# Two token tiles transposed by the matmul engine, and weight pieces moved out of the early tiles

## The chip, the cores and the metric

The kernel runs on one core of one Trainium2 chip. The metric is the device time of one execution in microseconds. The engines are PE (matmul), ACT (scalar), DVE (vector), POOL (gpsimd) and SP (here it only issues DMAs); each runs its own instruction stream, and semaphores order them against each other.

## The reference

Three layers follow each other: windowed attention with a summary of every block, a dense two-layer MLP, and a mixture of 8 experts of which every token takes one. The last is what the change is about:

```python
def _moe2_ref(x, w_gate, w1, w2):            # x 1536x512, w1 8x512x1024, w2 8x1024x512
    logits = x @ w_gate
    expert_idx = np.argmax(logits, axis=1)
    ...
    for e in range(E):
        mask = expert_idx == e
        ...
        h = np.maximum(x[mask] @ w1[e], 0.0)
        out[mask] = gate_w[mask, None] * (h @ w2[e])
```

With the inputs of these runs the experts get 879, 426, 168, 62 and 1 tokens, and three get none.

## The kernel before

The tokens form 12 tiles of 128 (u = 0 to 11). Float32 values are kept as a high and a low float16 part, so a product is three matmuls. `x2_out(u)` takes the finished sum of the dense layer of tile u (`x2ps`, PSUM), makes the two parts `x2c` (ACT L518 the high, DVE L519 the low), transposes them by DMA into `x2t` and stores them in `x2d` in DRAM. `gate(u)` multiplies `x2t` by the gate weights (L537, 12 matmuls into `pl`), finds the expert of every token and its slot by some 20 short DVE operations and one ACT operation, and POOL writes token number and gate value into `tbl`. A planner's list of positions (`at`) sets the order in which the program is written here, and within it the framework schedules each engine's stream.

The mixture follows in `sparse()`. The experts are ranked; (v, j) is tile j of the expert of rank v. The expert of rank 0 has 426 tokens, three full tiles and a half tile of 64 or fewer; rank 1 has seven full tiles; ranks 2 to 4 have one full tile and a half one, a half one, a half one. Three tiles of rank 0, (0,0) to (0,2), are the early tiles: they run on tables made before the last gates, and an If (`redo`, L886) repeats them when too few tokens were known. Then come `last_half(0)`, a chain of branches (`go`, L877) for further tiles of rank 0 that is jumped over here, `full(1, 0)`, and `chain(1, 1)` for (1,1) to (1,6); the ranks behind follow.

`s_tile` is one tile: 96 matmuls L715 into two PSUM halves `hp`, after each half ACT L719 and DVE L720 make `hh`, then (`work`) the weight pieces, then 24 matmuls L734 into `yp` (L730 for a half tile), ACT L737 scales it to `y`, and POOL L740 writes the rows to `out_dram`. `gather` and `h_gather` get a tile's rows: POOL L685 gathers from `x2d` into `xr`, and SP L687 transposes by DMA into `xa`, `xb`, `xe` or `xh`.

An expert's weights come in 8 pieces of 512 KB. Piece g belongs to the expert of rank g // 8. `piece(g)` splits it from one of five buffers `raw0` to `raw4` into two float16 parts (`s_split`: ACT L197, then DVE L198), and then has SP load piece g + 5 into the buffer it freed (`s_load`, L661 and L664). The buffers hold pieces 22 (= SOON) to 26 when the early tiles begin: 22 in `raw2`, 23 in `raw3`, 24 in `raw4`, 25 in `raw0`, 26 in `raw1`. `prep(lo, hi)` is the list of pieces lo to hi - 1, and `beside[j]` the first piece that is done in tile (1, j). `prep_x(r)` gathers the first tiles of rank r and loads the table of rank r + 1. On ACT and DVE a tile with `work` keeps the written order.

## Time and profile before

| what | value |
|---|---|
| median of 3 runs | 565.43 us (564.78 to 569.46) |
| the profiled execution | 564.62 us, of which 562.8 us from the first to the last instruction |
| mean granted PE clock | 0.926 |
| PE busy | 476.8 us, 85% of the span |
| DVE, ACT, POOL busy | 303.6, 264.0 and 223.2 us |
| DMA | 87.49 MB, 155 GB/s in the mean |

The profiled execution is 0.81 us under the median. Starts are in microseconds from the begin of the span. [...]

### The profile page before, as it was taken

The page shows a single profiled execution, that of the slowest core. Times are in us where ns is not written, and L with a number is a line of the kernel's source. Part 1 is how long each engine was busy: PE and PEld are TensorE (multiplying, and loading weights), DVE is VectorE, ACT ScalarE, POOL GpSimd, SP SyncE. Part 2 cuts the span into 40 slices and gives each one's busy share as a digit, 9 for nine tenths or more (in the row PEclk, how much of TensorE's full clock was granted, in tenths as well). Part 3 has the DMA queues.
Part 4 walks back from the last instruction along what each step waited for, and adds up shares of the span by engine and source line. Part 5 has one row for each costly group of instructions (what it writes and reads, how often), then busy time and mean ns, then how long its engine had stood idle before and what let it go on. Part 6 is the DMA issues. An engine that isn't in the chain of part 4 may idle for free.

```text
span 562.8 us, 12709 instructions
## 1 busy us (share of the span) xinstructions
PE 476.8 (85%) x4792; PEld 325.2 (58%) x4792; DVE 303.6 (54%) x778; ACT 264.0 (47%) x559; POOL 223.2 (40%) x217
## 2 busy tenths in 40 slices
PE   5726957969899999999999997989938799996971
PEld 2315844847556555686587476547617476775650
DVE  5999699998972233573354268865332344310110
ACT  3777685877774233356266235644132344321110
POOL 3476765777674113465156206501301332210110
PEclk9856995899999999999999998999988899997997
DMA  8997967995650454714351558884394999940310
GB/s 276 263 249 200 322 192 165 207 232 162 180 139 0 76 94 108 158 40 88 83 94 24 103 155 254 270 254 127 131 174 86 271 278 324 207 124 21 46 35 7
DMA packets 114775, 87.49 MB, mean 155 GB/s; under 512 B 85199, under 2 KB 94671, under 8 KB 114688
## 3 DMA queue, kind: packets, MB, share of 16 engines
q1 hardware_dynamic: 104656, 65.27, 48.2%
q10 hardware_dynamic: 7056, 13.11, 7.8%
q0 software_dynamic: 2976, 8.01, 4.6%
q8 instruction: 47, 0.77, 0.6%
q14 instruction: 40, 0.33, 0.2%
HBM read 57.29 MB, written 7.97 MB: 116 GB/s over the span
## 4 chain that ended last, share of the span: by engine, by line
PE 31%; DMA 30%; DVE 16%; issue 16%; POOL 2%; ACT 2%; SPq 1%; POOLq 1%; another core or an unknown queue 0%; ACTq 0%; DVEq 0%
PE x2ps L510 16%; PE hps L490 11%; DMA xr<-x2d,tbh 7%; DMA out_dram<-y,tbe 6%; DMA xr<-x2d,tb 4%; DMA stg<-in_moe_w_in_dram 2%; DMA tbl<-row,slot 2%; DVE yps L234 2%; DVE y L238 2%; DVE yps L236 2%; DVE s L401 2%; DMA pt<-pb 2%; DVE kb L198 2%; PE ps L385 2%; PE po L443 1%
## 5 line engine op out<-in xcount | busy, mean ns | idle before, releaser
L490 PE MATMUL hps<-xt,wih 128*128 128x256 f16 x768 | 137.0, 283 | 10.4 <-DVE rel L496 5.7
L510 PE MATMUL x2ps<-wo,gt 128*128 128x512 f16 x576 | 131.2, 380 | 0.0
L490 PE MATMUL hps<-xt,wil 128*128 128x256 f16 x384 | 108.8, 283 | 2.8 <-POOL wil L247 2.8
L490 PEld LDWEIGHTS <-wih 128*128 128x128 f16 x768 | 76.7, 102 | 24.8 <-issue 4.7
L510 PEld LDWEIGHTS <-gt 128*128 128x128 f16 x576 | 54.9, 98 | 60.5
L501 POOL TENSOR_TENSOR gt<-rel,gt 128x512 f16<-128x512 f32 x48 | 56.6, 1185 | 39.9 <-ACT gt L500 39.6
L715 PEld LDWEIGHTS <-w1t 128*128 128x128 f16 x1152 | 61.9, 100 | 17.0 <-DVEq L886 9.0
L720 DVE SCALAR_TENSOR_TENSOR hh<-hp,hh 128x512 f16<-128x512 f32 (+1 forms) x30 | 18.6, 618 | 83.4 <-ACT hh L719 76.1
L734 PE MATMUL yp<-w2t,hh 128*128 128x512 f16 x240 | 56.4, 387 | 3.9 <-ACT hh L719 3.3
L719 ACT ACTIVATE hh<-hp 128x512 f16<-128x512 f32 (+1 forms) x30 | 16.2, 540 | 70.0 <-PE hp L715 57.8
L496 DVE SCALAR_TENSOR_TENSOR rel<-rel,hps 128x512 f32<-128x512 f32 x48 | 32.6, 680 | 27.9 <-ACT rel L495 27.8
L411 ACT ACTIVATE s<-s,nm 128x184 f32<-128x184 f32 x88 | 38.2, 436 | 19.1 <-DVE nm L406 18.5
L490 PEld LDWEIGHTS <-wil 128*128 128x128 f16 x384 | 39.0, 102 | 11.0 <-POOL wil L247 2.9
L734 PEld LDWEIGHTS <-hh 128*128 128x128 f16 x264 | 25.2, 99 | 33.8 <-ACT hh L719 4.3
L495 ACT ACTIVATE rel<-hps,brelu 128x512 f32<-128x512 f32 x48 | 32.5, 676 | 17.0 <-PE hps L490 11.1
L715 PE MATMUL hp<-xb,w1t 128*128 128x128 f16 x672 | 38.7, 219 | 1.7 <-DVEq L877 1.7
L500 ACT ACTIVATE gt<-rel 128x512 f16<-128x512 f32 x48 | 29.8, 624 | 19.9 <-DVE rel L496 19.7
L421 POOL TENSOR_TENSOR pb<-s,pb 128x512 f16<-128x512 f32 x22 | 26.0, 1180 | 31.1 <-issue 22.7
L385 PEld LDWEIGHTS <-qt 64*128 64x128 f16 x576 | 19.1, 102 | 24.6 <-issue 9.1
L573 POOL DMA_INDIRECT tbl<-row,slot x12 | 12.8, 1067 | 48.5 <-DVE slot L567 47.8
L740 POOL DMA_INDIRECT out_dram<-y,tb x8 | 8.8, 1102 | 56.7 <-ACT y L737 39.7
L385 PE MATMUL ps<-kb,qt 64*128 64x160 f16 x288 | 19.4, 259 | 10.2 <-DVE nm L401 7.0
(189 smaller groups left out, 783.7 us busy)
## 6 DMA issues: line engine op xcount, KB each, us to landing
raw<-in_moe_w_dram SPq DMA_DIRECT2D x23, 512.0 KB
eraw<-in_moe_w_dram SPq DMA_DIRECT2D x22, 512.0 KB
stg<-in_moe_w_out_dram ACTq DMA_DIRECT2D x16, 512.0 KB
stg<-in_moe_w_in_dram ACTq DMA_DIRECT2D x9, 512.0 KB
x2d<-x2c SPq DMA_DIRECT2D x12, 256.0 KB
vraw<-in_v_dram SPq DMA_DIRECT2D x11, 256.0 KB
qraw<-in_q_dram SPq DMA_DIRECT2D x10, 256.0 KB
ek<-in_k_dram SPq DMA_DIRECT2D x3, 512.0 KB
```

The costliest lines, as they stand in the source:

```text
L385: nc.tensor.matmul(out=ps[i % 2][:, o + c0:o + c1], lhsT=qt[u][p, a, h // 2, :], rhs=keys[p, c, h // 2, :], start=(j == 0), stop=(j == 2))
L411: nc.scalar.activation(s[:, i, :], s[:, i, :], AF.Exp, bias=nm[:, i:i + 1], accum_out=sums[u][:, 4 * g + i:4 * g + i + 1])
L421: nc.gpsimd.tensor_tensor(out=p[:, :, 256:384], in0=s[:, :, 0:c1], in1=p[:, :, 0:c1], op=ALU.subtract)
L490: nc.tensor.matmul(out=hps[:, c, :], lhsT=w[:, kk, f:f + 128], rhs=xt[j][:, a * KD + kk, :], start=(i == 0), stop=(i == 3 * KD - 1))
L495: nc.scalar.activation(r, hf, AF.Relu, scale=S_G / (S_X * S_WI) ** 2, bias=brelu)
L496: nc.vector.scalar_tensor_tensor(out=r, in0=r, scalar=6.0 * S_G / (S_X * S_WI), in1=hf, op0=ALU.min, op1=ALU.mult)
L500: nc.scalar.activation(gh, r, AF.Copy)
L501: nc.gpsimd.tensor_tensor(out=gl, in0=r, in1=gh, op=ALU.subtract)
L510: nc.tensor.matmul(out=o, lhsT=gts[j][:, a, f, i * 128:(i + 1) * 128], rhs=w[:, f, :], start=(f == 0 and n == 0), stop=(f == KF - 1 and n ...
L715: nc.tensor.matmul(out=hp[:, c, :], lhsT=w1t[:, a, kk, f:f + 128], rhs=x[:, b * KD + kk, 0:n], start=(i == 0), stop=(i == 3 * KD - 1))
L720: ve.scalar_tensor_tensor(out=hh[:, 1, m * 4:m * 4 + 4, :], in0=hp, scalar=0.0, in1=hi, op0=ALU.max, op1=ALU.subtract)
L734: nc.tensor.matmul(out=yp, lhsT=hh[:, a, f, :], rhs=w2t[:, b, f, :], start=(f == 0 and i == 0), stop=(f == FK - 1 and i == 2))
```

## The change

Tiles 10 and 11 are transposed by PE (`pe_transpose`, which the kernel has for other tiles, L445 to L451: eight transposes of 128x128 into PSUM and one DVE copy) where a DMA did it. The early tiles carry no weight pieces, and the loop that did pieces between `last_half(0)` and `chain(0, n)` is gone; pieces 22 on are done in the tiles of rank 1, with 4, 4, 4, 3 and 3 pieces in (1,0) to (1,4) where 3, 3, 3, 2 and 2 were. A condition in a catch-up loop that these inputs don't enter changes too. Lines after the first edit move down by 4 or 5.

```diff
         t = x2p.tile([128, 2 * KD, 128], F16, tag="x2t", name="x2t")
-        nc.sync.dma_start_transpose(out=t, in_=xf)
+        if u < TILES - 2:
+            nc.sync.dma_start_transpose(out=t, in_=xf)
+        else:
+
+            pe_transpose(t, xf)
         nc.sync.dma_start(out=x2d[u * 128:(u + 1) * 128, :], in_=xf)
...
         for vj in early_tiles:
-            s_tile(*vj, work=prep(SOON, 8 * EARLY) if vj == early_tiles[-1] else ())
+            s_tile(*vj)
...
-        beside = [8 * EARLY + i for i in (3, 6, 9, 12, 14, 16)]
+
+        beside = [SOON + i for i in (0, 4, 8, 12, 15, 18)]
...
         last_half(0)
-        for f in prep(8 * EARLY, beside[0]):
-            f()
         chain(0, n)
...
-                with tc.If(nt[1] <= 2 * j + 1), tc.If(nt[3 if j == 1 else 4] > 0):
+                with tc.If(nt[1] <= 2 * j + 1), tc.If(nt[3 if j < 3 else 4] > 0):
```

The DVE stream around gate 10 before, from the low part of tile 10 to the low part of tile 11 (`gmx` and `gca` are gate values):

```order
L519 SCALAR_TENSOR_TENSOR x2c_4974<-x2ps_4897,x2c_4974 128x512
L198 SCALAR_TENSOR_TENSOR w2t1_4423<-eraw_4429,w2t1_4423 128x1024
L198 SCALAR_TENSOR_TENSOR wih_120<-eraw_4429,wih_120 128x1024 x2
L543 TENSOR_REDUCE gmx_5023<-pl_5010 128x1
L544 SCALAR_TENSOR_TENSOR gca_5024<-pl_5010,gmx_5023,cf_113 128x8
L552 TENSOR_SCALAR gmx_5023<-gmx_5023 128x1
L519 SCALAR_TENSOR_TENSOR x2c_5004<-x2ps_4949,x2c_5004 128x512
```

The result of gate 10 (L543) follows the two splits of `wih` directly. The same place of the DVE stream now:

```order
L519 SCALAR_TENSOR_TENSOR x2c_4974<-x2ps_4897,x2c_4974 128x512
L198 SCALAR_TENSOR_TENSOR w2t1_4423<-eraw_4429,w2t1_4423 128x1024
L198 SCALAR_TENSOR_TENSOR wih_120<-eraw_4429,wih_120 128x1024 x2
L451 COPY x2t_4977<-ptr_4978 128x1024
L547 TENSOR_REDUCE gmx_5041<-pl_5028 128x1
L548 SCALAR_TENSOR_TENSOR gca_5042<-pl_5028,gmx_5041,cf_113 128x8
L556 TENSOR_SCALAR gmx_5041<-gmx_5041 128x1
L519 SCALAR_TENSOR_TENSOR x2c_5013<-x2ps_4949,x2c_5013 128x512
```

The copy of the transposed tile 10 stands behind the two splits of `wih`, ahead of the first operation on the gate's result.

The ACT stream from the last early tile's `hh` on, before; the last two rows are pieces 24 and 25, ahead of the redo branch:

```order
L719 ACTIVATE hh_5507<-hp_5508 128x512
L719 ACTIVATE hh_5507<-hp_5559 128x512
L197 ACTIVATE wil_121<-raw2_5320 128x1024
L197 ACTIVATE wil_121<-raw3_5321 128x1024
L737 ACTIVATE y_5618<-yp_5617,tbe0_4427 128x512
L197 ACTIVATE w1u_5316<-raw4_5322 128x1024
L197 ACTIVATE w1u_5316<-raw0_5318 128x1024
```

All four of these pieces have left this place. ACT's (1,0) before, from the end of the skipped tiles, with piece 26 ahead of `hh` and pieces 27 to 29 behind it:

```order
L877 UNCONDITIONAL_BRANCH x10
L197 ACTIVATE w1u_5316<-raw1_5319 128x1024
L719 ACTIVATE hh_7552<-hp_7553 128x512
L719 ACTIVATE hh_7552<-hp_7604 128x512
L197 ACTIVATE w1u_5316<-raw2_5320 128x1024
L197 ACTIVATE w2u_5317<-raw3_5321 128x1024
L197 ACTIVATE w2u_5317<-raw4_5322 128x1024
L737 ACTIVATE y_7666<-yp_7665,tb1_5324 128x512
```

None of these four pieces is in (1,0) any more. ACT's (1,0) now:

```order
L723 ACTIVATE hh_7552<-hp_7553 128x512
L723 ACTIVATE hh_7552<-hp_7604 128x512
L197 ACTIVATE wil_121<-raw2_5338 128x1024
L197 ACTIVATE wil_121<-raw3_5339 128x1024
L197 ACTIVATE w1u_5334<-raw4_5340 128x1024
L197 ACTIVATE w1u_5334<-raw0_5336 128x1024
L741 ACTIVATE y_7669<-yp_7668,tb1_5342 128x512
```

Pieces 22 to 25 moved from the early tile behind the two `hh` of (1,0), and piece 26 to (1,1).

SP's DMAs in (1,0) before, from the last-half table of rank 2 on, with tables and rows of the next tiles between the weight loads (the rows that read registers are not shown):

```order
L793 DMA tbh2_5333<-tbl_58 64x2
L661 DMA raw2_5320<-in_moe2_w1_dram 128x1024
L664 DMA raw3_5321<-in_moe2_w2_dram 128x2x512
L664 DMA raw4_5322<-in_moe2_w2_dram 128x2x512
L664 DMA raw0_5318<-in_moe2_w2_dram 128x2x512
L687 DMA_TRANSPOSE xb2_5343<-xr0_5349 128x8x128
L664 DMA raw1_5319<-in_moe2_w2_dram 128x2x512
L679 DMA tb3_5326<-tbl_58 128x24
L793 DMA tbh3_5334<-tbl_58 64x2
L687 DMA_TRANSPOSE xh1_5345<-xr1_5350 128x8x64
L687 DMA_TRANSPOSE xe00_4424<-xr1_5351 128x8x128
L687 DMA_TRANSPOSE xh2_5346<-xr0_5348 128x8x64
```

Four weight loads stand here ahead of the transpose of `xb2`, and a fifth behind it. The same place of SP's stream now:

```order
L683 DMA tb2_5343<-tbl_58 128x24
L797 DMA tbh2_5351<-tbl_58 64x2
L683 DMA tb3_5344<-tbl_58 128x24
L797 DMA tbh3_5352<-tbl_58 64x2
L691 DMA_TRANSPOSE xb2_5361<-xr0_5367 128x8x128
L691 DMA_TRANSPOSE xh1_5363<-xr1_5368 128x8x64
L691 DMA_TRANSPOSE xe00_4424<-xr1_5369 128x8x128
L691 DMA_TRANSPOSE xh2_5364<-xr0_5366 128x8x64
L665 DMA raw2_5338<-in_moe2_w1_dram 128x1024
L668 DMA raw3_5339<-in_moe2_w2_dram 128x2x512
L668 DMA raw4_5340<-in_moe2_w2_dram 128x2x512
L668 DMA raw0_5336<-in_moe2_w2_dram 128x2x512
```

The loads of pieces 27 to 30 (`raw2`, `raw3`, `raw4`, `raw0`) stood ahead of the first transpose and now stand behind the fourth.

## Rows read from the trace of the kernel before

**Rows 1.** Timeline of PE, 405 to 458 us: start, duration, line, operation, count, [idle before <-releaser].
```profile
408.43 4.91 PE L734 MATMUL yp<-w2t,hh 128*128 128x512 f16 x22 [0.35 <-issue]
421.81 4.37 PE L715 MATMUL hp<-xh,w1t 128*128 128x64 f16 x96 [8.46 <-DVEq L886]
426.01 3.62 PE L730 MATMUL yp<-w2t,hh 128*128 128x512 f16 x16
431.29 5.53 PE L715 MATMUL hp<-xb,w1t 128*128 128x128 f16 x96 [1.66 <-DVEq L877]
...
442.31 4.27 PE L734 MATMUL yp<-w2t,hh 128*128 128x512 f16 x12 [2.90 <-ACT hh L719]
446.42 5.52 PE L715 MATMUL hp<-xb,w1t 128*128 128x128 f16 x96
451.78 5.34 PE L734 MATMUL yp<-w2t,hh 128*128 128x512 f16 x24
456.96 1.22 PE L715 MATMUL hp<-xb,w1t 128*128 128x128 f16 x19
```

**Rows 2.** Timeline of DVE, 408 to 424 us.
```profile
419.40 1.22 DVE L198 SCALAR_TENSOR_TENSOR w1u<-raw,w1u 128x1024 f16<-128x1024 f32 x1 [2.32 <-ACT w1u L197]
```

**Rows 3.** Windows: length, PE busy (instructions), granted clock, DMA share, GB/s.
```profile
421.80:424.80 3.00, 3.00 (x57) 0.50 0.07 12
...
442.31:446.42 4.11, 4.11 (x13) 0.62 1.23 326
...
535.89:538.85 2.96, 2.96 (x97) 1.00 0.27 100
```

**Rows 4.** Timeline of ACT, 404 to 482 us.
```profile
441.66 0.60 ACT L719 ACTIVATE hh<-hp 128x512 f16<-128x512 f32 x1 [6.80 <-remote]
...
443.85 1.06 ACT L197 ACTIVATE w2u<-raw 128x1024 f16<-128x1024 f32 x1 [0.65 <-DMA raw<-in_moe_w_dram]
445.67 1.06 ACT L197 ACTIVATE w2u<-raw 128x1024 f16<-128x1024 f32 x1 [0.76 <-DMA raw<-in_moe_w_dram]
...
457.70 1.06 ACT L197 ACTIVATE w1t<-raw 128x1024 f16<-128x1024 f32 x1 [3.23 <-DMA raw<-in_moe_w_dram]
...
475.36 0.60 ACT L719 ACTIVATE hh<-hp 128x512 f16<-128x512 f32 x1 [4.34 <-remote]
```

**Rows 5.** Timeline of all engines around the last two gates, 368 to 386 us.
```profile
367.77 7.93 PE L510 MATMUL x2ps<-wo,gt 128*128 128x512 f16 x36
...
371.33 0.68 DVE L519 SCALAR_TENSOR_TENSOR x2c<-x2ps,x2c 128x512 f16<-128x512 f32 x1
...
372.04 1.26 SPq L523 DMA_TRANSPOSE x2t<-x2c  x1
...
377.69 0.46 PE L537 MATMUL pl<-wg,x2t 128*128 128x8 f16 x12 [1.99 <-DMA x2t<-x2c]
377.72 1.22 DVE L198 SCALAR_TENSOR_TENSOR wih<-eraw,wih 128x1024 f16<-128x1024 f32 x1 [2.18 <-ACT wih L197]
...
384.60 0.46 PE L537 MATMUL pl<-wg,x2t 128*128 128x8 f16 x12 [1.07 <-DMA x2t<-x2c]
```

**Rows 6.** Tile `ptr`: count, duration ns min/median/max, first and last start.
```profile
L450 PE MATMUL ptr<-ch,xc x24: 219/259/314, 50.1 to 143.2; 128*128 128x128 f16 x24
L451 DVE COPY xt<-ptr x3: 669/679/691, 52.8 to 145.5; 128x1024 f16<-128x1024 f16 x3
```

**Rows 7.** Timeline of SP's DMA issues, 425 to 456 us.
```profile
436.52 2.84 SPq L664 DMA_DIRECT2D raw<-in_moe_w_dram  x3
440.08 4.02 SPq L687 DMA_TRANSPOSE xb<-xr  x1
...
449.32 1.94 SPq L687 DMA_TRANSPOSE xh<-xr  x1
452.24 1.56 SPq L661 DMA_DIRECT2D raw<-in_moe_w_dram  x3
```

**Rows 8.** Timeline of POOL, 420 to 500 us.
```profile
435.70 0.95 POOL L685 DMA_INDIRECT xr<-x2d,tb  x1 [3.32 <-DMA tb<-tbl]
```

## The prediction

> **What bounds the kernel now.** PE is busy in 85% of the span, so what can be won is where it stands still; I looked for that in PE's own timeline first, and then followed the releasers to the other engines'. Around the changed code there are three. After the last early tile PE ends at 413.34 and starts half(0) only at 421.81, 8.46 us idle, and the releaser is the vector engine's queue at the redo branch [rows 1]. The same vector engine runs its last weight subtract at 419.40, for 1.22 us, so it gets to that branch at 420.62 [rows 2]. That subtract belongs to piece 25, whose load set its time: PE waits for weights it won't use for 50 us. The second place is 1.66 us before (1,0) at 431.29. The third is inside (1,0): its second half waits 2.90 us for ACT's hh, and then runs at a clock of 0.62 [rows 1, 3]. ACT's hh came late because ACT itself waited 6.80 us on something called remote, right after its jump over the skipped tiles [rows 4]. So (1,0) took 15.13 us, from 431.29 to 446.42, against 10.54 for the tile behind it (446.42 to 456.96) [rows 1].

> [...]

> In the gate stage PE waits 1.99 us before gate 10 and 1.07 us before gate 11, both for a transpose by DMA [rows 5].

> **Part 1: the gates.** Removed are two DMA transposes on SP, the first with 1.26 us of issue. From the end of the subtract that fills x2c (371.33 + 0.68 = 372.01) to gate 10 it was 5.68 us; the wait at its end, 1.99, is all that PE can win there [rows 5].

> Added for each tile are eight PE transposes and one vector copy. The only rows for them are early in the kernel: 259 ns median for one transpose, 679 ns for the copy [rows 6]; 8 x 0.259 = 2.07 at most, and by 8 x 0.08 = 0.6 if they overlap like other 128-wide matmuls do (96 in 5.53 us is 58 ns each [rows 1]; I allow a third more). I take 0.6 for PE's time. Where they stand matters more. PE reaches those of u=10 in the middle of the accumulation of u=11, at about 370.4 by my reckoning from its 48 matmuls, which end at 375.70 (36 of them took 7.93 us, 0.22 each [rows 5]; half stand behind the transposes, 24 x 0.22 = 5.3); the first half of x2c comes from ACT and the second only from the subtract that ends at 372.01. So PE stalls up to 1.1 us and then needs 0.6: the accumulation of u=11 ends 1.7 later. On the vector engine the copy is queued behind the second wih subtract, 377.72 + 1.22 = 378.94 [rows 5]; this subtract waits for ACT's copy of a weight load, and PSUM holds the transposes meanwhile. So gate 10 would go to 378.94 + 0.68 = 379.6; if that load lands somewhat earlier, since one transpose less is on the DMA queues, to 378.1. I take 379.0, against 377.69. Gate 11 has 1.07 us of wait to win, and its copy follows gate 10's short operations. From gate 10 to the end of the first half of hp(0,0) I put 7.2 in place of 7.4. Sum of part 1: +1.0, from -0.3 (both waits won, only stall lost) to +2.0. That delay moves counts and ranking, on which tables and gathers of the first expert hang.

> [...]

> **Part 2: no weights in the early tiles.** ACT's and the vector engine's pieces 22 to 25 leave the place before the redo branch. The vector engine then passes the branch after its subtract of (0,2), about 412, and PE's own end decides: 413.34 plus 1.0 of part 1, and some 1.3 for the branches (1.19 = 421.81 - 420.62 is what PE took after the subtract [rows 1, 2]). So half(0) starts at 415.6, not 421.81. The gather and transpose for xh0 are long done then. With a clock that has had no time to fall it takes 2.96 + 3.62 = 6.6 instead of 7.82 [rows 1, 3]. (1,0) then needs about 1.7 of branching: 423.9 against 431.29, so -7.4. Its operand xb0 was fetched beside the early tiles. Without piece 26 ahead of it and without four weight loads issued in its middle, its 2.90 of stall and the low clock after it (4.27 us for 12 matmuls, at 0.62, where 24 take 5.34 [rows 1, 3]) go: another -4.5. By this alone (1,1) begins at 434.5 and (1,2) at 445.0, not 456.96: -12.

> **Part 3: what is given back.** The loads of pieces 27 to 30 start only when 22 to 25 have been split, which is now in (1,0), and on SP they are queued behind four transposes, those of xb2, xh1, xe00 and xh2. Before, they were issued at 436.52 (three of them, 2.84 us), ahead of the first transpose at 440.08 [rows 7]. These transposes wait for gathers on POOL, and the first gather was at 435.70 [rows 8]. By the order of the program it stands behind SP's jump over the skipped tiles, and SP gets there behind the load of piece 26, which follows the last gather of the first expert in both kernels. So I leave the gather at 435.7, the first transpose at 440.1, and the last, xh2, whose issue was 1.94 us [rows 7], ends at 444.5 to 446. Four loads follow. A first load issued at 452.24 was split at 457.70, 5.46 later [rows 4, 7]; loads issued in a row were split 1.82 apart (443.85, 445.67) [rows 4]. From 445.2: piece 27 lands at 450.7, 28 at 452.5, 29 at 454.3 (452.5 to 456).

> ACT has to split 26 to 29 in (1,1), in written order, ahead of y(1,1) and of hh of (1,2). PE finishes the first matmuls of (1,2) at about 450.5, and then waits. After piece 29: 1.06 for the ACT copy, 0.67 for y, 0.60 for hh, and about 0.5 for the vector engine's half of hh, 2.85 in all; the 24 second matmuls, 5.34 us [rows 1] when PE has been busy but here starting at a lower clock after an idle stretch, I put at 6.75. So (1,2) ends at 454.3 + 2.85 + 6.75 = 463.9, where it ended at 456.96 + 10.54 = 467.50. From -12 are left **-3.6**. The pieces behind keep up: piece 33 would land near 462, and is needed before hh of (1,3) at about 466.7. Everything behind, up to the last output, moves along, since there PE runs tile on tile.

> **The sum.** The profiled execution took 564.62 us, 0.81 below the median of 565.43. 564.62 - 3.6 = 561.0.

> **Rivals.**
> A: the third tile is not held, because the gathers come sooner or the loads land faster (29 by about 446). For: half(0) and its output are 6 us earlier, and the first gather waited also for that output. Against: the load of piece 26 at its old place, and the four transposes ahead of the loads. Then the 12 us stay: 564.62 - 12 = 552.6.

> B: ACT's remote wait returns where PE has no slack. The trace has two, 6.80 us and 4.34 us [rows 4]. If one of 4.3 falls on an hh behind (1,2) with PE waiting for it, it comes on top of 561.0: 565.3. For: both stand behind branches of ACT, and the changed kernel has the same branches. Against: a wait in (1,0) or (1,1) is covered by the wait for piece 29. [...]

> C, the one that ends slower: the weights don't catch up. Four pieces a tile are 2 MB in 10.54 us. If a batch of four loads and its transposes take as long as (1,0) did, 15.13 us, the tiles (1,3) and (1,4) are each held by 4.6: 561.0 + 9.2 = 570.2. It decides once piece 33 lands later than about 466. Against: before, with three pieces a tile, ACT already waited 3.23 us for a load at 457.70 [rows 4], and (1,1) and (1,2) ran on without a gap on PE [rows 1].

> D: the transposes don't help but hurt by their whole 2.0, or win their 0.3: +1.0 or -1.3 on the above if the third tile isn't held by loads, almost nothing if it is, since the loads then set its end. This lies in the range.

> **How the numbers follow.** Forecast 0.55 (559.0 to 563.5, by piece 29 between 452.5 and 456 and the clock after it), A 0.23 (552 to 555), B 0.15, C 0.07. A measurement of this kernel can tell about 1% from no change: below 559.8 is faster, above 571.1 slower. Faster: A and a third of the forecast's own range, 0.41. Slower: the upper part of C and what lies beyond, 0.05. The rest is 0.54. The range takes in the forecast, B and most of A: 553.0 to 566.5; left out are C, the bottom of A and the ends. The forecast's own range is 559.0 to 563.5.

> **What the changed kernel's profile would show.** PE's half(0) between 415 and 416.5 with no wait on the redo branch, at a clock near 1.00; (1,0) at about 424 and 10.5 long. The transposes by PE in the middle of the second-layer sum of u=11, with a wait of about 1 us, and gate 10 near 379. SP's load of piece 27 behind xh2, at 444 to 446. In (1,2) a wait of PE for ACT of 4 to 8 us behind ACT's wait for raw, then a clock of 0.5 to 0.7; no such wait in (1,3). I would be wrong if (1,2) has no wait (A), if the gates cost more than 2 us, if PE waits before half(0) on something the early weights had hidden (xh0, its weights, ACT), or if loads wait tile after tile (C).

## The result, and the profile after

The changed kernel took **559.16 us** (median of 20 runs, 552.67 to 566.33) against 565.2 us (20 runs, 561.72 to 569.46): the medians lie 6.0 us apart. The ratio is 0.9864, interval [0.9838, 0.9889], or 7.7 us (6.3 to 9.2) less; it leaves out the slower ones of these executions. The forecast was 561.0, range 553.0 to 566.5. The profiled execution is one of the fastest of the 20: 553.73 us, span 551.8, mean granted clock, as a share of full speed, 0.939. So 11 us lie between the two profiles and 6 between the medians; rows must be read with that in mind.

PE's timeline of the changed kernel, where [rows 1] stood (start, duration, line, operation, count, [idle before <-releaser]):

```profile
407.57 5.34 PE L738 MATMUL yp<-w2t,hh 128*128 128x512 f16 x24
414.05 0.66 PE L719 MATMUL hp<-xh,w1t 128*128 128x64 f16 x17 [1.14 <-DMA raw<-in_moe_w_dram]
418.48 4.37 PE L719 MATMUL hp<-xh,w1t 128*128 128x64 f16 x79 [3.77 <-issue]
...
428.40 5.53 PE L719 MATMUL hp<-xb,w1t 128*128 128x128 f16 x96 [1.74 <-DVEq L882]
...
438.95 5.52 PE L719 MATMUL hp<-xb,w1t 128*128 128x128 f16 x96
...
449.49 5.52 PE L719 MATMUL hp<-xb,w1t 128*128 128x128 f16 x96
456.11 0.60 PE L738 MATMUL yp<-w2t,hh 128*128 128x512 f16 x2 [1.10 <-ACT hh L723]
456.91 4.92 PE L738 MATMUL yp<-w2t,hh 128*128 128x512 f16 x22 [0.19 <-DVE hh L724]
461.67 5.52 PE L719 MATMUL hp<-xb,w1t 128*128 128x128 f16 x96
```

half(0) starts at 414.05, 7.8 us earlier than in [rows 1], and no longer waits for the vector engine at the redo branch. But it stops after 17 of its 96 first matmuls, for 3.77 us, with nothing but issue as the reason, and (1,0) comes at 428.40, only 2.9 earlier. (1,0) and (1,1) run through in 10.55 each. (1,2) is held for 1.10 and 0.19 us and ends at 461.67. The window behind the stop (columns as in [rows 3]):

```profile
418.50:421.50 3.00, 3.00 (x58) 0.50 0.60 170
```

What holds (1,2) is on ACT, in the place of [rows 4]:

```profile
450.14 1.06 ACT L197 ACTIVATE w1u<-raw 128x1024 f16<-128x1024 f32 x1 [4.09 <-DMA raw<-in_moe_w_dram]
451.49 1.06 ACT L197 ACTIVATE w2u<-raw 128x1024 f16<-128x1024 f32 x1 [0.29 <-DMA raw<-in_moe_w_dram]
453.94 1.06 ACT L197 ACTIVATE w2u<-raw 128x1024 f16<-128x1024 f32 x1 [1.39 <-DMA raw<-in_moe_w_dram]
454.90 0.67 ACT L741 ACTIVATE y<-yp,tb 128x512 f32<-128x512 f32 x1
```

and on SP, in the place of [rows 7]:

```profile
442.65 1.19 SPq L691 DMA_TRANSPOSE xh<-xr  x1
444.11 0.36 SPq L665 DMA_DIRECT2D raw<-in_moe_w_dram  x1
444.72 2.10 SPq L668 DMA_DIRECT2D raw<-in_moe_w_dram  x3
```

The four loads follow the fourth transpose, from 444.11 on, and piece 29 is there at 453.94. ACT splits it, then makes y, and only then hh for (1,2).

The gates, where [rows 5] stood:

```profile
370.11 0.58 ACT L518 ACTIVATE x2c<-x2ps 128x512 f16<-128x512 f32 x1
...
372.12 0.53 PE L450 MATMUL ptr<-ch,x2c 128*128 128x128 f16 x4 [0.98 <-DVE x2c L519]
...
377.81 1.23 DVE L198 SCALAR_TENSOR_TENSOR wih<-eraw,wih 128x1024 f16<-128x1024 f32 x1 [2.17 <-ACT wih L197]
378.96 0.68 DVE L451 COPY x2t<-ptr 128x1024 f16<-128x1024 f16 x1
...
379.70 0.46 PE L541 MATMUL pl<-wg,x2t 128*128 128x8 f16 x12 [0.32 <-DVE x2t L451]
...
384.15 0.44 PE L541 MATMUL pl<-wg,x2t 128*128 128x8 f16 x12
```

The copy does wait behind the second wih subtract, and gate 10 is at 379.70, 9.59 us after ACT began on the output of tile 10 (370.11).

Of the 11.0 us between the two profiles 5.9 lie between the start of tile 10's output and the start of (1,3); 4.6 more lie where the forecast had none, at the end of the second expert and in half(2). PE there, before:

```profile
505.35 5.34 PE L734 MATMUL yp<-w2t,hh 128*128 128x512 f16 x24
514.92 5.28 PE L715 MATMUL hp<-xh,wih 128*128 128x64 f16 x96 [4.23 <-issue]
...
523.70 5.52 PE L715 MATMUL hp<-xe,wih 128*128 128x128 f16 x96
```

and after:

```profile
498.99 5.34 PE L738 MATMUL yp<-w2t,hh 128*128 128x512 f16 x24
506.44 2.96 PE L719 MATMUL hp<-xh,wih 128*128 128x64 f16 x96 [2.11 <-PEq L888]
...
512.70 5.52 PE L719 MATMUL hp<-xe,wih 128*128 128x128 f16 x96
```

The last matmul of the second expert, in its tile (1,6), ends at 505.35 + 5.34 = 510.69 and 498.99 + 5.34 = 504.33. From there to (2,0), the row with xe, it was 13.01 us and is 8.37. The gap shrank from 4.23 to 2.11, and the 96 matmuls of half(2) from 5.28 to 2.96 us. In the gap of before, the only traffic between 512 and 513 us was this (queue, packets, MB, share of 16 engines):

```profile
DMA packets 1, 0.02 MB, mean 16 GB/s; under 512 B 0, under 2 KB 0, under 8 KB 0
...
q8 instruction: 1, 0.02, 5.9%
```

One packet of the instruction queue, 0.02 MB, and 1.9 us after that stretch PE went on. In the changed kernel such a packet moved during the stop within half(0) (414.7 to 418.5 us), beside other transfers:

```profile
q8 instruction: 1, 0.02, 1.5%
```

The profile does not say for which engine an instruction packet is, and a packet alone proves no wait; the padded kernels below say more.

### The profile page after: what moved, and what is told of

Read it like the earlier page. It is cut to its first block, busy times and chain, and to the rows that moved or that the text cites. A ratio compares the mean times of both kernels' runs of the same rounds, so it can differ in the third digit from the quotient of the medians.

```text
span 551.8 us, 12743 instructions
## 1 busy us (share of the span) xinstructions
PE 475.2 (86%) x4808; PEld 323.4 (59%) x4808; DVE 305.5 (55%) x780; ACT 263.2 (48%) x559; POOL 224.6 (41%) x217
## 5 line engine op out<-in xcount | busy, mean ns | idle before, releaser
L510 PE MATMUL x2ps<-wo,gt 128*128 128x512 f16 x576 | 133.0, 383 | 0.3 <-POOL gt L501 0.3
L738 PE MATMUL yp<-w2t,hh 128*128 128x512 f16 x240 | 54.4, 379 | 1.5 <-ACT hh L723 1.1
L723 ACT ACTIVATE hh<-hp 128x512 f16<-128x512 f32 (+1 forms) x30 | 16.1, 539 | 52.3 <-PE hp L719 43.6
L577 POOL DMA_INDIRECT tbl<-row,slot x12 | 12.8, 1068 | 51.8 <-DVE slot L571 51.1
L385 PEld LDWEIGHTS <-qt 64*128 64x128 f16 x576 | 17.7, 98 | 23.9 <-issue 8.4
L385 PE MATMUL ps<-kb,qt 64*128 64x160 f16 x288 | 17.9, 244 | 10.6 <-DVE nm L401 7.9
```

The costliest lines, as they stand in the source:

```text
L385: nc.tensor.matmul(out=ps[i % 2][:, o + c0:o + c1], lhsT=qt[u][p, a, h // 2, :], rhs=keys[p, c, h // 2, :], start=(j == 0), stop=(j == 2))
L510: nc.tensor.matmul(out=o, lhsT=gts[j][:, a, f, i * 128:(i + 1) * 128], rhs=w[:, f, :], start=(f == 0 and n == 0), stop=(f == KF - 1 and n ...
L738: nc.tensor.matmul(out=yp, lhsT=hh[:, a, f, :], rhs=w2t[:, b, f, :], start=(f == 0 and i == 0), stop=(f == FK - 1 and i == 2))
```

## The experiments

Several profiles show that the output of tile 10 itself comes at 369.6 to 375.3 us, in stages that no kernel here changes. So I compare two stretches within a profile: **a**, from ACT's start on the output of tile 10 (L518) to the first matmul of (1,3), which holds the gates, the early tiles, half(0) and the first three tiles of the second expert; and **b**, from the end of the second expert's last matmul to the first of (2,0). Each row has a and b of one profile; the median is that of the kernel's timed runs, the ratio that against the kernel before on the same chip. The last column says after how many of the 96 first matmuls of half(0) PE stopped; where it is empty PE waited for the vector engine ahead of half(0) and then ran through.

| kernel | median us | ratio, interval | a | b | hp of half(0) stops after |
|---|---|---|---|---|---|
| before | 565.2 | | 97.44 | 13.01 | |
| before_again | 566.4 | 1.0033 [0.9994, 1.0072] | 95.14 | 12.85 | |
| pad_4 | 562.8, one run | | 96.86 | 11.65 | |
| pad_32 | 563.3, one run | | 95.16 | 8.43 | |
| before_pad | 559.54 | 0.9867 [0.9818, 0.9915] | 93.87 | 8.41 | |
| pe_only | 561.58 | 0.9939 [0.9897, 0.9981] | 92.62 | 8.41 | |
| weights_only | 563.72 | 0.9970 [0.9933, 1.0007] | 92.85 | 12.14 | 34 matmuls |
| weights_pad | 558.53 | 0.9838 [0.9781, 0.9895] | 92.12 | 9.96 | 18 |
| after | 559.16 | 0.9864 [0.9838, 0.9889] | 91.56 | 8.37 | 17 |
| after_again | 558.35 | 0.9870 [0.9814, 0.9926] | 94.09 | 8.39 | 17 |
| no_redo | 559.07 | 0.9815 [0.9745, 0.9884] | 94.08 | 9.89 | none |
| keep_two | 555.63 | 0.9814 [0.9753, 0.9875] | 91.86 | 8.41 | 17 |
| keep_two_again | 558.28 | 0.9917 [0.9884, 0.9949] | 91.47 | 8.41 | 17 |
| keep_two_pad | 557.04 | 0.9872 [0.9843, 0.9901] | 89.21 | 9.91 | 18 |

**The changed kernel again.** No edit.

> The changed kernel once more, for a second profile. Theory W (the weight move is the gain: half(0) no longer waits for the last split, (1,0) loses its stall, and the late loads give part back in (1,2)): ratio 0.984 to 0.990, and again PE reaches half(0) near 414, is stopped within it for 2 to 4 us with nothing but issue as the reason, and (1,2) is held 1 to 3 us. Theory F (most of the 11 us between the two profiles is chance in when the instruction pieces arrive, above all before half(2)): the gap before half(2), 2.1 us in the first profile of the changed kernel and 4.2 in that of the kernel before, is about 4 here, and the span is nearer 556 than 552.

The ratio is the first one's, the stop in half(0) was 2.07 us, and b is 8.39 a second time: the short gap before half(2) is no chance of the first profile. Theory F was wrong in that, but right in the span, 556.9. (1,2) was held 0.19 us only and not 1 to 3, since here the second expert began late, at 433.79.

**Only the transposes by PE**: the first hunk of the change alone.

> Only the transposes by PE, the weight pieces where they were. Theory W: nothing to be seen, ratio 0.997 to 1.002; the last early tile ends 0.2 to 0.6 us earlier, near 412.9, but half(0) still waits for the last split and starts at 421 to 422. Rival G (the gates give a good part of the gain): ratio 0.992 to 0.995, and half(0) starts 2 to 4 us earlier than 421.8.

The ratio is the rival's, its reason hardly: half(0) started at 425.80, behind the vector engine as before. Counted from ACT's start on the output of tile 10, which came late here (375.33), that is 50.5 us, against 51.8 and 52.3 in the two profiles of the kernel before, so 1.3 to 1.8 earlier and not 2 to 4. Most of the gain sits in b, 8.41, which neither theory had in it.

**Only the weight pieces moved**: the change without its first hunk.

> Only the weight pieces moved, tiles 10 and 11 still transposed by DMA. Theory W: ratio 0.985 to 0.990, as the whole change; half(0) starts at 414 to 415.5. Rival G: ratio 0.991 to 0.995, since the gates' part is missing.

This spoke against theory W: 0.997 instead of 0.985 to 0.990. half(0) started 0.97 us after the last early tile, but stopped like this:

```profile
419.48 1.15 PE L715 MATMUL hp<-xh,w1t 128*128 128x64 f16 x34 [0.96 <-PEq L887]
424.13 3.49 PE L715 MATMUL hp<-xh,w1t 128*128 128x64 f16 x62 [3.50 <-issue]
```

Here it ran 34 matmuls before the stop, where the change had 17. A matmul is two PE instructions, a weight load and the multiplication (4808 of each in the profile of the changed kernel): 17 x 2 = 34 instructions, within one matmul of the 16 x 2 = 32 that the transposes add to PE's stream ahead of it. So PE stops at one fixed place of its program; weights_pad, keep_two and keep_two_pad below fit that too, with 17 or 18 matmuls.

**Pieces 22 and 23 left in the last early tile**:

```diff
-            s_tile(*vj)
+            s_tile(*vj, work=prep(SOON, 8 * EARLY) if vj == early_tiles[-1] else ())
...
-        beside = [SOON + i for i in (0, 4, 8, 12, 15, 18)]
+        beside = [SOON + i for i in (2, 5, 8, 12, 15, 18)]
```

> The whole change, but pieces 22 and 23 stay in the last early tile; 24 to 26 are done in (1,0), three pieces each in (1,0) and (1,1). Theory W: it was pieces 24 and 25, whose loads land late, that held the redo branch, so half(0) starts within 1 us of the changed kernel's; two loads are issued early and (1,2) is held less: ratio to the changed kernel 0.996 to 1.001. Rival H (any piece beside the early tiles holds half(0)): half(0) starts 2 us or more later than in the changed kernel, ratio to it 1.003 or more.

half(0) started 1.11 us after the early tiles' end (after: 1.14), so pieces 24 and 25 were what held the redo branch, not 22 and 23. The ratio is 0.994 of the changed kernel's on the same chip (after_again), a little below what I expected. In (1,2) PE waited for nothing:

```profile
450.93 5.52 PE L719 MATMUL hp<-xb,w1t 128*128 128x128 f16 x96
456.29 5.34 PE L738 MATMUL yp<-w2t,hh 128*128 128x512 f16 x24
461.47 5.52 PE L719 MATMUL hp<-xb,w1t 128*128 128x128 f16 x96
```

**The kernel before again.** No edit.

> The kernel before once more, for a second profile of it. Ratio 0.996 to 1.004. If the gap before half(2), with nothing but issue as its reason and the lower clock behind it, belongs to the program (theory P, the position of PE's code), it is again 4 to 4.6 us here and (2,0) starts 12 to 13 us after the second expert's last tile, against 8.4 in all three kernels with the transposes by PE. If it is chance, it is near 2.1 in one of two.

b is 12.85, so the long gap belongs to that program. The stall of (1,0) does not:

```profile
427.18 4.24 PE L715 MATMUL hp<-xh,w1t 128*128 128x64 f16 x96 [10.66 <-DVEq L886]
...
436.54 5.53 PE L715 MATMUL hp<-xb,w1t 128*128 128x128 f16 x96 [1.66 <-DVEq L877]
...
447.09 5.52 PE L715 MATMUL hp<-xb,w1t 128*128 128x128 f16 x96
```

436.54 to 447.09 is 10.55 us. The wait of ACT for remote of 6.80 us [rows 4] was one of that execution.

**16 idle transposes in the kernel before**:

```diff
+        if u >= TILES - 2:
+            z = ps_h.tile([128, 2 * KD, 128], F16, tag="h", name="pad")
+            for c in range(2 * KD):
+                nc.tensor.transpose(out=z[:, c, :], in_=ch[:, H_ID:H_ID + 128], identity=ch[:, H_ID:H_ID + 128])
         nc.sync.dma_start_transpose(out=t, in_=xf)
```

> The kernel before, with 16 more transposes by PE of a constant, 8 in the output of tiles 10 and 11 each, whose result nobody reads: as many PE instructions more as the change brings, and no gate is served by them. Theory P (the 32 PE instructions more move the later code against the places where PE has to get the next piece of its program): the gap before half(2) falls from 4.2 to 2.1, (2,0) starts 8.4 us after the second expert, ratio 0.991 to 0.995, as with the transposes alone. Theory G (the gates' shorter way is the gain of the transposes): the gap stays at 4.2 or more and the ratio is 0.998 to 1.004.

Theory P, and more than it said. Work that serves nothing gives 0.9867, as much as the whole change, where 0.991 to 0.995 was expected. By the interval that is 4.8 to 10.3 us, and b accounts for 4.4 to 4.6 of it; where the rest comes from is not shown. The end of the second expert reads as in the changed kernel:

```profile
504.05 5.34 PE L738 MATMUL yp<-w2t,hh 128*128 128x512 f16 x24
511.55 2.96 PE L719 MATMUL hp<-xh,wih 128*128 128x64 f16 x96 [2.16 <-PEq L887]
```

**The same 16 with the weight pieces moved.**

> Only the weight pieces moved, with the same 16 idle transposes. Theory P: as the whole change, 0.984 to 0.990, PE stops after 17 matmuls of half(0) instead of 34, and the gap before half(2) is 2.1. Theory G: as the weight move alone, 0.994 to 1.000.

Theory P again: 0.9838, with the whole change's 0.9864 and 0.9870 inside its interval. Whether the 16 transposes serve the gates or nothing makes no difference that these runs can tell.

**4 and 32 idle transposes**: the same edit, with 4 in tile 11 only, and with 16 in each of both tiles. From 91 to 401 us, ahead of the branches, the instruction queue moved 21 packets while PE ran 5351 matmuls and weight loads in the kernel before and 5371 in the changed one: a packet for every 254.8 and 255.8. The steps of 256 in the first expectation are close to that.

> The kernel before with 4 idle transposes, 8 PE instructions, in the output of tile 11. Theory P, with a step and not a slope: PE's stop in half(0) came after 34 matmuls without and 17 with the 32 instructions more, so a piece of the program ends at one fixed place in the instruction stream, and counted on in steps of 256 the next such place lies between the last tile of the second expert and half(2) in the kernel before, and still does with 8 more: the gap before half(2) stays at 4 to 4.6 us. A rival by which any added work helps would give a gap between 2.1 and 4.

> The kernel before with 32 idle transposes, 64 PE instructions. Theory P: the place has moved into the last tile of the second expert, as with 32 instructions: gap before half(2) 2.1 us and its 96 matmuls in 2.96 us.

pad_4 and then pad_32, at the end of the second expert:

```profile
504.89 5.34 PE L738 MATMUL yp<-w2t,hh 128*128 128x512 f16 x24
514.32 4.27 PE L719 MATMUL hp<-xh,wih 128*128 128x64 f16 x96 [4.08 <-PEq L887]
```

```profile
508.30 5.34 PE L738 MATMUL yp<-w2t,hh 128*128 128x512 f16 x24
515.82 2.96 PE L719 MATMUL hp<-xh,wih 128*128 128x64 f16 x96 [2.18 <-PEq L887]
```

8 instructions change little in the gap (4.08 against 4.23 and 4.47 in the kernel before), 32 and 64 bring it to 2.16 and 2.18. The single times, 562.8 and 563.3 us, tell nothing.

Where is the place? Count PE's instructions in the order of the program. In weights_only, as in the kernel before, the matmuls of half(0) begin at 7275, and PE stopped in front of 7343, 34 matmuls on; in all seven profiles with a stop it is 7343, to the instruction. With the step of 254.8 to 255.8 instructions measured above, I estimate the 16th such place behind 7343 at 11420 to 11436, an estimate good to some tens of instructions. Before, the last matmul of (1,6) is 11435, so the place lies near it; what follows in the program, (1,7) and half(1), is jumped over here, and half(2) begins at 11950. (The expectation of pad_4 puts the place between the last tile and half(2); by this estimate it lies at the end of the last tile.) Every instruction more ahead moves the end of (1,6) one further behind that place: 8 in pad_4, 32 with the idle transposes (35 with the real ones), 64 in pad_32. As I read it, with 32 or more the packet can be asked for while (1,6) still runs.

The packets of the instruction queue, of 16384 bytes each, agree. In the four profiles with the long gap one began 2.18 to 2.71 us ahead of the end of (1,6) (2.63 in the kernel before); in the eight with 32 or 35 instructions more, and in no_redo below, it was 4.71 to 5.42 (5.15 in the changed kernel), in pad_32 6.44. A second followed 3.0 to 4.3 us later. In the ten profiles with the short gap this second one was there before the gap began; in the four others it ended within the gap, and PE went on 1.94 to 2.27 us later (1.95 in the kernel before). In all seven stops within half(0), PE went on 1.36 to 1.46 us after the end of such a packet (1.42 in the changed kernel). The queue also keeps step with PE in the tiles of the second expert: from 444.88 on the packets of the changed kernel come 10.96, 11.14 and 11.58 us apart, and at 240 matmuls and weight loads in a tile of 10.54 that is 250, 254 and 264 of them. That PE waits for the packet fits all of this; the profile does not name the queue's engine. In half(0) PE did not stop at the jump, but 17 or 34 matmuls behind it.

**Without the redo branch**: the If that repeats early tiles is left out, with what it computes and with the hint on this branch that the program gives PE ahead of the early tiles.

```diff
-        tc.mark_branch_hint_location("redo", hint="LikelyTaken", engines=[ET.PE])
...
-        with tc.If(done <= len(early_tiles), label="redo"):
...
-                    s_tile(0, j)
```

> The changed kernel without the branch that repeats early tiles when too few tokens were known (left out; these inputs don't enter it). PE then runs from (0,2) into half(0) without a jump over that code. Theory J (the stop of 2 to 4 us within half(0) is PE waiting for the next piece of its program behind a jump): the stop goes, half(0) takes 6.6 us, (1,0) starts 9 to 10.5 us after the end of (0,2) instead of 12.8 to 15.5, ratio to the changed kernel 0.991 to 0.996. Rival (the stop comes from a load or an operand): it stays at 2 us or more.

```profile
415.12 2.96 PE L719 MATMUL hp<-xh,w1t 128*128 128x64 f16 x96
417.92 3.62 PE L734 MATMUL yp<-w2t,hh 128*128 128x512 f16 x16
423.28 5.53 PE L719 MATMUL hp<-xb,w1t 128*128 128x128 f16 x96 [1.74 <-DVEq L881]
...
459.36 7.33 PE L738 MATMUL yp<-w2t,hh 128*128 128x512 f16 x24 [9.47 <-ACT hh L723]
```

The stop is gone, half(0) takes 2.96 + 3.62 and (1,0) starts at 423.28, as theory J had it (8.00 us after the early tiles, even less than it said). The edit also shifts the later code, but not out of the way: half(0) begins at 6808 here, and the place two of the steps above ahead of 7343 is 6831 to 6833, about 12 matmuls into this half(0); PE ran over it. So, as far as that estimate holds, the place alone does not stop PE, it takes the jump too; the hint that went with the branch was not tested by itself. But (1,2) then waits 9.47 us for ACT, which waited for a weight load:

```profile
454.18 1.06 ACT L197 ACTIVATE w1u<-raw 128x1024 f16<-128x1024 f32 x1 [13.25 <-DMA raw<-in_moe_w_dram]
```

(1,0) started 50.8 us after ACT's start on the output of tile 10 (372.45), against 58.3 and 61.1 in the two profiles of the change, and nothing of that was left at the end of (1,2): a is 94.08, against 91.56 and 94.09. The median, 559.07, is the changed kernel's; the ratios, 0.9815 here and 0.9864 there, have intervals that overlap, so the expected gain of 0.4 to 0.9% stays open.

**Two pieces kept, transposes by DMA, 16 idle ones; and two pieces kept again, on the same chip.**

> Pieces 22 and 23 kept in the last early tile, tiles 10 and 11 transposed by DMA as before, and 16 idle transposes for the position of PE's code. The trace said that the way by PE and the vector engine brings gate 10 some 2 us later after the output of tile 10 than the DMA did. If that reaches the end, this version beats the same with real transposes by 1 to 2 us: ratio 0.975 to 0.982. If the gates' delay is lost in later waits, it is equal to it.

> The whole change with pieces 22 and 23 kept in the last early tile, again, beside the one with idle transposes: ratio 0.978 to 0.985, and no wait of PE for ACT in (1,2).

557.04 against 558.28, with intervals that overlap (0.9872 and 0.9917, both above what was expected): it stays open whether the gates' delay reaches the end. PE in keep_two_pad:

```profile
448.76 5.52 PE L719 MATMUL hp<-xb,w1t 128*128 128x128 f16 x96
454.85 0.60 PE L738 MATMUL yp<-w2t,hh 128*128 128x512 f16 x2 [0.56 <-ACT hh L723]
...
468.40 0.60 PE L738 MATMUL yp<-w2t,hh 128*128 128x512 f16 x2 [2.29 <-ACT hh L723]
```

The wait that was gone from (1,2) is partly back there (0.56) and in (1,3) (2.29): weights that are not waited for in one tile are waited for in the next. keep_two_again shows the same, with nothing in (1,2) and 1.34 in (1,3). keep_two had 0.9814 in one set of runs and 0.9917 in the other, so I don't claim that it beats the change.

## Why the prediction was right, and where it was not

The time and its sign were right, in good part by luck. The forecast -3.6 stood for the weight move alone, which was worth less; a term that was not in the sum at all, the place of PE's later code, made up for it.

**The weight move was mis-sized**: forecast -3.6, about -2.5 in the profiles and -1.0 to -3.2 in the times. The six profiles with the pieces where they were have a = 92.62 to 97.44, mean 95.2; the four with them moved as in the change (weights_only, weights_pad, after, after_again) 91.56 to 94.09, mean 92.7. Three pairs differ by the move alone, on one chip each: weights_only is 1.0 us under the kernel before, weights_pad 1.0 under before_pad, after_again 3.2 under pe_only (medians). The ratio of weights_only, 0.997 [0.9933, 1.0007], allows between nothing and 3.8 us. Within it:
- "PE's own end decides", half(0) at 415.6: right, 414.05. The step that failed is "with a clock that has had no time to fall it takes 6.6". PE was stopped for 3.77 us behind 17 matmuls, and 79 matmuls then took 4.37 us at 0.50; from start to end half(0) took 12.61. The kernel before has the same jump and place and did not stop: there two instruction packets moved between 416.38 and 419.42, under the wait for the vector engine, which therefore, as I read it, hid the stop. Without the branch it does take 6.6, at a granted clock of 1.00 from 415.1 to 418.0, and (1,0) starts at 423.28, for which I had 423.9.
- "Its 2.90 of stall and the low clock [...] go: another -4.5": the stall went, but it was a chance of one execution, absent in before_again. It should not have been in the sum at all.
- "What is given back": the mechanism held. SP's loads follow the fourth transpose (forecast 444.5 to 446, seen 444.11), piece 29 was there at 453.94 (forecast 454.3), and PE waits for ACT in (1,2). Since (1,0) came late, the hold was small in the profile after (1.29 us); where (1,0) came on time, in no_redo, it was 9.47. In no_redo the loads alone set the end of (1,2), as the sum said. Counted from ACT's start on the output of tile 10 that end was forecast at 93.8 (463.9 - 370.06); seen were 91.56 and 94.09 in the change, where PE came to it late and waited 1.29 and 0.19 us, and 94.08 in no_redo.
- "Weights it won't use for 50 us" was too short a time, which changes nothing in the sum: piece 25 is a weight of rank 3 (`w1u`), whose first matmul came at 535.89, 115 us behind.

**The gates**: forecast gate 10 at 379.0, that is 1.3 later; the copy did queue behind the wih subtract. From ACT's start on the output of tile 10 it takes 7.63 us before and 9.59 after, so 2.0 later, the upper end of what I had for the part; to the end of the early tiles it is 41.0 to 44.7 us (median 41.8) in the eight profiles with DMA and 42.8 to 48.3 (44.4) in the six with PE. That this costs time at the end isn't shown: weights_pad and the change are equal within their intervals. Gate 10 came at 9.12 to 9.73 us in the six profiles with PE, at 7.05 to 7.63 in the eight with DMA; gate 11 at 13.50 to 15.74 and 13.97 to 14.83, so there is no gain to be seen there either. What the transposes brought, 0.9939 alone, comes with before_pad too.

**What was missed**: "everything behind moves along". b has a mean of 12.4 (11.65 to 13.01) in the four profiles with up to 8 PE instructions more, and of 8.7 (8.37 to 9.96) in the nine with 32 or 64 more (no_redo, with other code ahead, is left out), so -3.7. It comes from no edit as such but from the place of later code in PE's instruction stream. In the times, the 32 instructions brought 3.2 us (pe_only against before), 5.4 (after_again against weights_only) and 6.5 (before_pad against before), each on one chip: the larger part of the 6.0. That -2.5 and -3.7 make -6.2 is a sum of means over few profiles, and closes better than they allow.

**The rivals.** A, no hold: seen in keep_two, not in the change. B, the remote wait: it came back in some executions (4.44 us in after_again, 3.55 in weights_only, 3.78 in pe_only), and PE lost 0.45 us to it in after_again. C, weights that don't catch up: only traces of it, 0.17 us in (1,3) after and up to 2.29 with two pieces kept.

**Still open**: what the weight move alone is worth beyond its interval; why before_pad gained more than b shows; whether DMA transposes with idle instructions beat the transposes by PE; and why the output of tile 10 comes up to 5 us apart from execution to execution.

## What to carry to other kernels

When an edit adds instructions ahead of code with taken branches, time a version that adds as many idle ones: if that gives the same gain, the edit's reason is not shown as the cause, and the position can be had for less. A stall that stands in one profile is no term of a sum until a second profile of the same kernel shows it. And before a wait is removed, look for what else would be waiting there: here a stop of PE of 2.07 to 4.0 us showed once its wait for the weights was gone, and in no_redo, without that stop, it waited 9.47 us for the weights themselves.
